# Where the first three transposed groups of each 512-token block are asked for

## The chip, the cores and the metric

One core of a Trainium2 chip runs the whole program. The metric is the device time of one execution in microseconds (us), as a median over several runs. The profile is of one execution of its own.

## The reference

```
p_packed = sm_attn(p, k, v)              # 8 batches, 8 heads, 576 tokens, head 64, 32 packs
x = sm_attn(q, p_packed, p_packed)       # -> 4608 tokens x 512
h = x @ w_in                             # 512 -> 1024
solu = h * softmax(h)
ln = (solu - mean) / sqrt(var + 1e-06) * g_ln
y = ln @ w_out                           # 1024 -> 512
m = max(y @ w1, y @ w2, y @ w3)          # 512 -> 768
out = m @ w_out2                         # 768 -> 512
```

Inputs and output are float32. Every matrix product outside the attention is made from operands split into a high and a low part, three matmuls for one.

## The kernel before, in words

The program has two stages. The first, up to some 530 us, makes the attention, `h`, the normalised activations and `y`. The second makes the three maxed products and the last product (lines 884 and 1146), and is a long run of matmuls. The change lies in the first.

**Tiles and blocks.** The 4608 tokens are 36 tiles of 128 (the loop `for t in range(nt)`, L1035). Four tiles are a block of 512 tokens, nine blocks in all. For each tile `tok_hidden` makes `h` (12 matmuls into two banks of PSUM, L633), and then VectorE and ScalarE turn it into `u`, the normalised activations, in a chain: the negated row maximum `nm` (L639, VectorE), the exponential (L641, ScalarE), the product `u` with its sum (L643, VectorE), `nmu` (L645), the squares (L647, ScalarE), the powers (L651 to L658, VectorE), and the final scaling of `u` (L659, ScalarE). When the four tiles of a block have their `u`, `y_transpose(j, kc)` transposes one group: the 128 columns number `kc` of the four `u` tiles, four 128x128 transposes on TensorE into one bank of PSUM (L700). ScalarE takes the high part from it (`lh`, L706), VectorE the low part (`ll`, L707), and the bank is free. There are eight groups in a block. `y_product` (L712) uses the group `kc` in two steps, one for each half of the output, six matmuls each (L725): 16 steps for a block.

**Banks.** The pool `ps_t` has four banks with one tag. The transposed groups share them with `mp` (L474, two banks for a set, evicted to `Mh` and `Ml`, L311 and L312), with `st` (L507, two banks for a set, evicted by two transposes of VectorE, L513), and with the transposes of queries and keys (L394, L488). `h` has two banks of its own.

**The order of work.** Each tile goes through a string of letters, for blocks in the middle `DFNTAHTTyTyDyTAFy`. `H` is `tok_hidden` of the tile itself; `y` brings the previous block's `y` to step 4i+4 at tile i of its block; `T` asks for one more transposed group of the previous block, if fewer than three are ahead of the `y` steps (`look=3`); `F` is a step of the attention of a later batch (`mp`, `st` and the VectorE work on it: `mx` L517, the difference L518, `sm` L521 to L523, `x` L524, the transposes L537); `D`, `W` and `A` are pieces of decoding weights (`dt` and `raw`, L123 to L139). Behind the fourth tile of each block, L1090 asks for the first three groups of that block at once. The order in which each engine then receives its instructions is set by a list scheduler. It is fixed when the program is built.

The seven places where this differs in the change are the ends of the tiles 7, 11, 15, 19, 23, 27 and 31. They are called the borders 1 to 7 here. They lie in the trace near 142, 193, 250, 301, 357, 408 and 458 us.

Of the kernel before, what the change touches and what calls it, by code (L numbers as in the profile page):

```python
# [57 lines left out]
def kernel(  # L58
# [155 lines left out]
    def decode_w_out(n, raw):  # L214

        t = lt_p.tile([P, TB], F32, tag="lh", name="dt")
        wt = lt_p.tile([P, TB], F32, tag="ll", name="wt")
        for f in decode(wt, raw, t, wt if CFG['l1'] == 'g' else None, ENG[CFG['d1']]):
            f()
        wv = wt.rearrange("r (k f) -> r k f", k=2)  # L220
        nc.scalar.copy(woh[:, 2 * n:2 * n + 2, :HM], wv)
        nc.gpsimd.tensor_tensor(
            out=wol[:, 2 * n:2 * n + 2, :HM], in0=wv, in1=f32(woh[:, 2 * n:2 * n + 2, :HM]), op=ALU.subtract
        )
        ready.update({(0, 2 * n), (0, 2 * n + 1)})

    def decode_w_out2(kc):

        t, start, rest = decode_piece(words(w_out)[kc * P:(kc + 1) * P, HM:, :])

        def arithmetic():
            rest()
            nc.scalar.copy(woh[:, kc, HM:], t)
            nc.gpsimd.tensor_tensor(out=wol[:, kc, HM:], in0=t, in1=f32(woh[:, kc, HM:]), op=ALU.subtract)
            ready.add((1, kc))

        return start, arithmetic
# [13 lines left out]
    def decode_w2(w, dst, r0, f):  # L251
        t, start, rest = decode_piece(words(w)[r0:r0 + P, f:f + DC, :])

        def arithmetic():
            rest()
            nc.sync.dma_start(out=dst[r0:r0 + P, f:f + DC], in_=t)

        return start, arithmetic
# [58 lines left out]
    nt = NT // P  # L317
# [652 lines left out]
    def load_w_out():  # L970
        if left:
            n = left.pop(0)
            raw = u_p.tile([P, DFF], F32, tag="u", name="raw").bitcast(I32)
            src = words(w_out)[2 * n * P:2 * (n + 1) * P, :HM, :]
            nc.sync.dma_start(
                out=raw.rearrange("r (k c) -> r k c", k=2), in_=src.rearrange("(k r) f t -> r k (f t)", r=P)
            )
            raws.append((n, raw.rearrange("r (f t) -> r f t", t=2)))
# [15 lines left out]
    def filler():  # L994
        if fill:
            fill.pop(0)()

    def need(t):
        for _, _, b, _ in parts_of(t):
            while not packed[b].done.issuperset(('M1', f'X{unit_of(b, t % tiles)}')):  # L1000
                filler()
# [6 lines left out]
    def finish():  # L1008

        for f in dec.pop(0):  # L1010
            f()

    def step_y(j, most):
        n = done.get(j, 0)
        if j >= 0 and n < most:
            while divmod(n, KFF) not in ready:
                if n < KFF:
                    if not raws:
                        load_w_out()
                    decode_w_out(*raws.pop(0))  # L1020
                else:
                    while dec:
                        finish()
                    if divmod(n, KFF) not in ready:
                        dec.append([*decode_w_out2(todo2.pop(0))])
            y_product(j, n)
            done[j] = n + 1

    def step_t(j, most):
        n = turned.get(j, 0)  # L1030
        if j >= 0 and n < min(most, KFF):
            y_transpose(j, n)
            turned[j] = n + 1

    for t in range(nt):  # L1035
        if t == 4:
            first_h.close()
            ps_y = late.enter_context(tc.tile_pool(name="ps_y", bufs=1, space=PSUM, reuse_waits="tile"))
        j, i = t // 4 - 1, t % 4
        for x in CFG['s0'][t] if j < 0 else CFG['s3' if t >= CFG['t3'] else 's2' if j else 's1']:  # L1040
            if x == 'H':
                need(t)
                tok_hidden(t)
            elif x == 'D':
                while dec:
                    finish()
                if raws:
                    decode_w_out(*raws.pop(0))
                elif t >= CFG['th'] and not left:
                    if todo2:  # L1050
                        dec.append([*decode_w_out2(todo2.pop(0))])
                    elif todo:
                        dec.append([*decode_w2(*todo.pop(0))])
                    elif todo3:
                        todo3.pop(0)()
            elif x == 'W':
                while dec:
                    finish()
                if todo3:
                    todo3.pop(0)()  # L1060
            elif x == 'A':
                for d in dec:
                    if len(d) == 2:
                        d.pop(0)()
            elif x == 'F':
                filler()
            elif x == 'L':
                load_w_out()
            elif x == 'N' and t % tiles in (3, 8) and nxt < B:
                while fill:  # L1070
                    filler()
                nb = packed[nxt] = Packed(nxt)
                nb.load(0)
                nb.load(1)
                fill += nb.steps()
                nxt += 1
            elif x == 'y':
                step_y(j, 4 * i + 4)
            elif x == 'T':
                step_t(j, done.get(j, 0) + CFG['look'])  # L1080
        if t % tiles in (3, 8) and nxt < B and (j < 0 or 'N' not in CFG['s1']):
            while fill:
                filler()
            nb = packed[nxt] = Packed(nxt)
            nb.load(0)
            nb.load(1)
            fill += nb.steps()
            nxt += 1
            filler()
        if i == 3:  # L1090
            for _ in range(CFG['look']):
                step_t(t // 4, CFG['look'])
    while fill or todo or dec or todo3:
# [162 lines left out]
```

## Time and profile before

| what | us |
|---|---|
| median of three runs | 1087.03 (1086.87 to 1087.38) |
| the profiled execution, its own time | 1080.05 |
| span of the profile | 1078.3 |
| mean granted clock of TensorE | 0.988 |
| PE busy, whole span | 1035.2 |
| VectorE busy, whole span | 713.0 |

The profiled execution is 6.98 us shorter than the median of the runs. A difference worked out in the profile is therefore put on its own 1080.05 us, and the same difference on the median. What lies outside the span is 1.75 us.

### The profile page before, as it was taken

Reading aid. Unit: us, or ns where it says so; the run is one execution under the profiler, and the core shown is the slowest. Engines: PE = TensorE matmul, PEld = TensorE weight load, DVE = VectorE, ACT = ScalarE, POOL = GpSimd, SP = SyncE. Lnnn points to the kernel's source line nnn. Section 1 sums busy time; section 2 is a strip of 40 time slices with the busy share of each in tenths; the row PEclk is TensorE's granted clock in tenths of the full one; section 3 lists DMA queues with packets and bytes.
Section 4 is the critical chain, followed back from the end, with each engine's and each line's share of the span. In section 5 each row is a group of like instructions: output and inputs, shape, how many; then the busy total and the mean of one; then the engine's idle time right before and its main releaser. Section 6 shows DMA issues by size and latency. Waiting matters only on the chain.

```text
span 1078.3 us, 18180 instructions
## 1 busy us (share of the span) xinstructions
PE 1035.2 (96%) x6624; PEld 881.1 (82%) x6624; DVE 713.0 (66%) x1434; ACT 482.4 (45%) x938; POOL 275.6 (26%) x296
## 2 busy tenths in 40 slices
PE   7779999999999999999999999999999999999997
PEld 6547667676767777777998899999989999999996
DVE  4697896979787896756888646625735754662560
ACT  6597666666666666576233421321331142132113
POOL 3342321111111121142585510410230041031002
PEclk8899999999999999999999999999999999999999
DMA  8853536564554623346564644543444453433411
GB/s 260 189 131 97 162 101 180 139 163 139 136 158 138 185 87 98 104 135 240 179 232 160 190 129 125 158 129 123 147 138 139 147 176 109 127 118 117 126 50 59
DMA packets 139528, 154.28 MB, mean 143 GB/s; under 512 B 51888, under 2 KB 92336, under 8 KB 139440
## 3 DMA queue, kind: packets, MB, share of 16 engines
q1 hardware_dynamic: 139440, 153.14, 48.6%
q8 instruction: 52, 0.85, 0.3%
q14 instruction: 36, 0.29, 0.1%
HBM read 116.92 MB, written 36.18 MB: 142 GB/s over the span
## 4 chain that ended last, share of the span: by engine, by line
PE 51%; DVE 2%; issue 1%; POOL 1%; DMA 1%; ACT 1%; DVEq 0%; ACTq 0%; POOLq 0%
PE m L884 33%; PE o L1146 13%; PE y L725 4%; PE h L633 1%; DVE wt L784 1%; DMA wt<-wdram 0%; PE tp L700 0%; DVE r L892 0%; POOL w2l L757 0%; DMA wt<-wodram 0%; DVE kept L892 0%; ACT u L659 0%; POOL hl L948 0%; POOL t1l L852 0%; DVE t L834 0%
## 5 line engine op out<-in xcount | busy, mean ns | idle before, releaser
L725 PE MATMUL y<-lh,woh 128*128 128x512 f32 x288 | 118.0, 413 | 0.6 <-ACT lh L706 0.6
L725 PE MATMUL y<-ll,woh 128*128 128x512 f32 x288 | 115.0, 399 | 0.0
L725 PE MATMUL y<-lh,wol 128*128 128x512 f32 x288 | 114.2, 397 | 0.0
L892 DVE TENSOR_TENSOR u<-m,q 128x384 f32<-128x384 f32 x54 | 29.9, 554 | 126.4 <-PE m L884 65.5
L917 ACT COPY q<-m 128x384 f32<-128x384 f32 x54 | 26.0, 481 | 178.4 <-PE m L884 178.4
L948 POOL TENSOR_TENSOR hl<-cur,hh 128x384 fp32r<-128x384 f32 x36 | 40.7, 1133 | 235.7 <-ACT hh L947 235.7
L139 POOL TENSOR_TENSOR wt<-raw 128x256 f32<-128x256 f32 x56 | 35.6, 636 | 228.2 <-DVE raw L136 130.3
L1146 PE MATMUL o<-w2h,hl 128*128 128x512 f32 x216 | 84.7, 392 | 0.6 <-POOL hl L948 0.6
L1146 PE MATMUL o<-w2l,hh 128*128 128x512 f32 x216 | 84.4, 391 | 0.0
L1146 PE MATMUL o<-w2h,hh 128*128 128x512 f32 x216 | 84.1, 389 | 0.0
L633 PE MATMUL h<-Mh,ah 128*128 128x512 f32 x160 | 67.5, 422 | 2.0 <-DVE u L643 1.5
L633 PE MATMUL h<-Mh,al 128*128 128x512 f32 x160 | 65.3, 408 | 0.0
L725 PEld LDWEIGHTS y<-lh,woh 128*128 128x128 f32 x288 | 53.8, 188 | 14.0 <-issue 1.4
L633 PE MATMUL h<-Ml,ah 128*128 128x512 f32 x160 | 64.9, 406 | 0.0
L725 PEld LDWEIGHTS y<-lh,wol 128*128 128x128 f32 x288 | 54.2, 188 | 12.1
L884 PE MATMUL m<-b22h,s 128*128 128x384 f32 x216 | 63.6, 335 | 0.0
L884 PE MATMUL m<-t1h,s 128*128 128x384 f32 x216 | 63.6, 334 | 0.0
L884 PE MATMUL m<-t2h,s 128*128 128x384 f32 x216 | 63.5, 334 | 0.0
L884 PE MATMUL m<-t3h,s 128*128 128x384 f32 x216 | 63.5, 334 | 0.0
L725 PEld LDWEIGHTS y<-ll,woh 128*128 128x128 f32 x288 | 54.4, 189 | 10.9 <-issue 0.5
L892 DVE TENSOR_TENSOR kept<-r,kept 128x384 f32<-128x384 f32 x72 | 58.4, 812 | 2.4
L707 DVE SCALAR_TENSOR_TENSOR ll<-tp,g_sb,lh 128x512 fp32r<-128x512 f32 x72 | 52.1, 743 | 11.8 <-ACT lh L706 11.7
(209 smaller groups left out, 2749.9 us busy)
## 6 DMA issues: line engine op xcount, KB each, us to landing
s<-sdram SPq DMA_DIRECT2D x188, 256.0 KB, 2.9
kt<-in_k_dram SPq DMA_DIRECT2D x16, 576.0 KB, 5.3
vt<-in_v_dram SPq DMA_DIRECT2D x16, 576.0 KB, 4.8
ydram<-yt SPq DMA_DIRECT2D x36, 256.0 KB, 2.5
raw<-in_moe_w_dram SPq DMA_DIRECT2D x36, 256.0 KB, 2.8
b<-ydram SPq DMA_DIRECT2D x24, 384.0 KB, 4.3
out_dram<-ob SPq DMA_DIRECT2D x36, 256.0 KB, 2.0
qtl<-in_q_dram SPq DMA_DIRECT2D x56, 128.0 KB, 2.9
```

The source lines that it names most:

```text
L139: add.tensor_tensor(out=dst, in0=f32(hi), in1=f32(lo), op=ALU.add)
L633: nc.tensor.matmul(h[:, n, :], lhsT=x, rhs=m[:, g, n * 512:(n + 1) * 512], start=(i == 0), stop=(i == len(ops) - 1),)
L707: last[nc.vector] = nc.vector.scalar_tensor_tensor(out=ll, in0=tp, scalar=gc, in1=f32(lh), op0=ALU.mult, op1=ALU.subtract)
L725: nc.tensor.matmul(ys[half][m], lhsT=w[:, kc, ms], rhs=x, start=(kc == 0 and i == 0), stop=(kc == KFF - 1 and i == 2),)
L784: nc.vector.tensor_tensor(out=out, in0=x, in1=y, op=op)
L884: nc.tensor.matmul(out, lhsT=w, rhs=y, start=start and i == 0, stop=i == len(ops) - 1, skip_group_check=not start,)
L892: mark[0] = nc.vector.tensor_tensor(**what)
L917: mark[1] = nc.scalar.copy(q, ba)
L948: nc.gpsimd.tensor_tensor(out=hl, in0=t, in1=f32(hh), op=ALU.subtract)
L1146: nc.tensor.matmul(ops[i], lhsT=x[:, ts], rhs=w, start=(c == 0 and n == 0), stop=(c == KF2 - 1 and n == 2),)
```

## The change

The line that asks for three groups behind a block's fourth tile now does so only for the first block (t = 3) and the last (t = 35). For the seven blocks between, the first three `T` of the next tile's string find no group yet, and ask for them: the first ahead of `H` of that tile, the second and the third behind it, and ahead of the first `y`. Nothing is computed more or less.

```
-        if i == 3:
+        if i == 3 and (t == 3 or t == nt - 1):
             for _ in range(CFG['look']):
                 step_t(t // 4, CFG['look'])
```

VectorE at border 1, around the evictions of the first five groups. `ll` are the low parts of the groups, `nm`, `u` and `nmu` belong to the next tile, `x` and `sm2` to the attention, `dt` and `raw` to decoding. The groups four and five are `ll_1938` and `ll_1969` in both orders. Before:

```order
L707 SCALAR_TENSOR_TENSOR ll_1876<-tp_1870,g_sb_119,lh_1875 128x512
L523 RECIPROCAL sm2_1826<-sm2_1826 128x20
L131 SCALAR_TENSOR_TENSOR raw_1784<-raw_1784,dt_1786 128x256
L524 TENSOR_TENSOR x_1809<-x_1809,sm2_1826 128x640
L134 TENSOR_SCALAR dt_1786<-raw_1784 128x256
L537 STREAM_TRANSPOSE y_1835<-x_1809 128x320 x2
L136 SCALAR_TENSOR_TENSOR raw_1784<-raw_1784,dt_1786 128x256
L639 TENSOR_REDUCE nm_1910<-h_1897 128x1
L707 SCALAR_TENSOR_TENSOR ll_1938<-tp_1932,g_sb_119,lh_1937 128x512
L128 TENSOR_SCALAR dt_1887<-dt_1887 128x256
L707 SCALAR_TENSOR_TENSOR ll_1969<-tp_1963,g_sb_119,lh_1968 128x512
L643 SCALAR_TENSOR_TENSOR u_1912,su_1914<-h_1897,u_1912 128x1024
```

Now:

```order
L639 TENSOR_REDUCE nm_1892<-h_1879 128x1
L537 STREAM_TRANSPOSE y_1835<-x_1809 128x320 x2
L707 SCALAR_TENSOR_TENSOR ll_1912<-tp_1906,g_sb_119,lh_1911 128x512
L643 SCALAR_TENSOR_TENSOR u_1894,su_1896<-h_1879,u_1894 128x1024
L707 SCALAR_TENSOR_TENSOR ll_1921<-tp_1915,g_sb_119,lh_1920 128x512
L645 TENSOR_SCALAR nmu_1898<-su_1896 128x1
L707 SCALAR_TENSOR_TENSOR ll_1938<-tp_1932,g_sb_119,lh_1937 128x512
L128 TENSOR_SCALAR dt_1860<-dt_1860 128x256
L707 SCALAR_TENSOR_TENSOR ll_1969<-tp_1963,g_sb_119,lh_1968 128x512
```

The second and third group are now evicted behind the next tile's `nm`, and the tile's `u` (L643) stands ahead of the third, fourth and fifth group instead of behind the fifth.

TensorE at border 2, directly behind the last `y` steps of the block before. Before:

```order
L700 MATMUL tp<-ident,u 128x128 x12
L474 MATMUL mp<-w_in_sb,ppT 32x512 x8
L507 MATMUL st<-qT,ppT 32x320 x8
L633 MATMUL h<-Mh,ah 128x512
L633 MATMUL h<-Ml,ah 128x512
L474 MATMUL mp<-w_in_sb,ppT 32x512 x8
L507 MATMUL st<-qT,ppT 32x256 x8
```

Now:

```order
L474 MATMUL mp<-w_in_sb,ppT 32x512 x8
L507 MATMUL st<-qT,ppT 32x320 x8
L633 MATMUL h<-Mh,ah 128x512
L474 MATMUL mp<-w_in_sb,ppT 32x512 x8
L507 MATMUL st<-qT,ppT 32x256 x8
L633 MATMUL h<-Ml,ah 128x512
L633 MATMUL h<-Mh,al 128x512
L633 MATMUL h<-Mh,ah 128x512
L633 MATMUL h<-Ml,ah 128x512
L633 MATMUL h<-Mh,al 128x512
L700 MATMUL tp<-ident,u 128x128 x4
```

The twelve transposes no longer stand ahead of the two sets of `mp` and `st`: both sets come first, with one `h` product between them, and the first group follows behind the sixth `h` product.

VectorE at border 3, from the next tile's `nm` to the eviction of the fifth group. The fourth group is `ll_3308`, the fifth `ll_3339`; `u` is the next tile's, `raw` and `dt` belong to decoding, the rest to the attention. Before:

```order
L639 TENSOR_REDUCE nm_3280<-h_3267 128x1
L521 TENSOR_REDUCE sm2_3254<-x_3237 128x2x8
L707 SCALAR_TENSOR_TENSOR ll_3308<-tp_3302,g_sb_119,lh_3307 128x512
L522 TENSOR_SCALAR sm2_3254<-sm2_3254 128x2x8
L134 TENSOR_SCALAR dt_3486<-raw_3484 128x256
L523 RECIPROCAL sm2_3254<-sm2_3254 128x2x8
L643 SCALAR_TENSOR_TENSOR u_3282,su_3284<-h_3267,u_3282 128x1024
L524 TENSOR_TENSOR x_3237<-x_3237,sm2_3254 128x2x256
L645 TENSOR_SCALAR nmu_3286<-su_3284 128x1
L136 SCALAR_TENSOR_TENSOR raw_3484<-raw_3484,dt_3486 128x256
L537 STREAM_TRANSPOSE y_3261<-x_3237 128x256 x2
L707 SCALAR_TENSOR_TENSOR ll_3339<-tp_3333,g_sb_119,lh_3338 128x512
```

Now:

```order
L639 TENSOR_REDUCE nm_3262<-h_3249 128x1
L521 TENSOR_REDUCE sm2_3227<-x_3210 128x2x8
L707 SCALAR_TENSOR_TENSOR ll_3282<-tp_3276,g_sb_119,lh_3281 128x512
L522 TENSOR_SCALAR sm2_3227<-sm2_3227 128x2x8
L707 SCALAR_TENSOR_TENSOR ll_3291<-tp_3285,g_sb_119,lh_3290 128x512
L523 RECIPROCAL sm2_3227<-sm2_3227 128x2x8
L643 SCALAR_TENSOR_TENSOR u_3264,su_3266<-h_3249,u_3264 128x1024
L524 TENSOR_TENSOR x_3210<-x_3210,sm2_3227 128x2x256
L645 TENSOR_SCALAR nmu_3268<-su_3266 128x1
L707 SCALAR_TENSOR_TENSOR ll_3308<-tp_3302,g_sb_119,lh_3307 128x512
L537 STREAM_TRANSPOSE y_3234<-x_3210 128x256 x2
L707 SCALAR_TENSOR_TENSOR ll_3339<-tp_3333,g_sb_119,lh_3338 128x512
```

The second and third group (`ll_3282`, `ll_3291`) have moved in behind `nm`, `u` stands ahead of the fourth too, and the pieces of decoding (L134, L136, and L131 some rows ahead) have gone from the stretch; they come behind the fifth group now.

## Rows read from the trace of the kernel before

**Rows 1.** Part 1 of the page: busy time, share of the span and instructions.

```profile
PE 1035.2 (96%) x6624; PEld 881.1 (82%) x6624; DVE 713.0 (66%) x1434; ACT 482.4 (45%) x938; POOL 275.6 (26%) x296
```

**Rows 2.** Stretches: length, PE, PEld, DVE, ACT, POOL busy (count), PEclk, DMA share, GB/s.

```profile
140.00:150.00 10.00, 7.89 (x34) 6.17 (x33) 9.41 (x22) 7.19 (x12) 2.40 (x5) 0.83 0.27 93
193.00:213.00 20.00, 19.72 (x158) 12.45 (x157) 19.27 (x44) 13.25 (x28) 3.25 (x3) 1.00 0.51 136
250.00:270.00 20.00, 19.56 (x138) 12.71 (x137) 19.03 (x43) 12.35 (x23) 2.81 (x5) 1.00 0.48 136
357.00:377.00 20.00, 19.19 (x169) 14.03 (x169) 16.95 (x46) 13.68 (x26) 2.45 (x4) 1.00 0.70 191
```

**Rows 3.** TensorE's timeline, border 1: start, us, instruction, count, idle before and releaser.

```profile
142.78 0.55 PE L700 MATMUL tp<-ident,u 128*128 128x128 f32 x3 [1.75 <-DVE x L513]
143.69 1.33 PE L700 MATMUL tp<-ident,u 128*128 128x128 f32 x5 [0.36 <-ACT u L659]
```

**Rows 4.** Timeline of VectorE, border 1.

```profile
148.11 0.82 DVE L521 TENSOR_REDUCE sm<-x 128x20 f32<-128x640 f32 x1 [0.40 <-ACT x L519]
...
156.27 1.23 DVE L643 SCALAR_TENSOR_TENSOR u<-h,u 128x1024 f32<-128x1024 f32 x1 [0.35 <-ACT u L641]
```

**Rows 5.** Timeline of TensorE, border 2.

```profile
192.94 1.47 PE L700 MATMUL tp<-ident,u 128*128 128x128 f32 x12
194.34 1.04 PE L474 MATMUL mp<-w_in_sb,ppT 64*32 64x512 f32 x2
195.66 1.09 PE L474 MATMUL mp<-w_in_sb,ppT 64*32 64x512 f32 x14 [0.28 <-DVE ll L707]
...
197.68 0.50 PE L633 MATMUL h<-Mh,ah 128*128 128x512 f32 x1
```

**Rows 6.** Timeline of TensorE, the same set away from a border.

```profile
435.08 1.09 PE L474 MATMUL mp<-w_in_sb,ppT 64*32 64x512 f32 x16
...
436.64 0.50 PE L633 MATMUL h<-Mh,ah 128*128 128x512 f32 x1
```

**Rows 7.** Timeline of VectorE, border 2: decoding, attention.

```profile
200.66 0.42 DVE L131 SCALAR_TENSOR_TENSOR raw<-raw,dt 128x256 int32<-128x256 int32 x1
...
204.86 0.28 DVE L134 TENSOR_SCALAR dt<-raw 128x256 int32<-128x256 int32 x1
...
205.25 0.36 DVE L136 SCALAR_TENSOR_TENSOR raw<-raw,dt 128x256 f32<-128x256 uint32 x1
...
210.24 0.67 DVE L517 TENSOR_REDUCE mx<-x 128x16 f32<-128x512 f32 x1
...
211.08 0.68 DVE L518 TENSOR_TENSOR x<-x,mx 128x512 f32<-128x512 f32 x1
```

**Rows 8.** Timeline of TensorE, border 3.

```profile
251.57 1.04 PE L474 MATMUL mp<-w_in_sb,ppT 64*32 64x512 f32 x2
...
254.68 0.50 PE L633 MATMUL h<-Mh,ah 128*128 128x512 f32 x1
```

**Rows 9.** Timeline of TensorE, border 7.

```profile
461.88 0.55 PE L700 MATMUL tp<-ident,u 128*128 128x128 f32 x3 [1.36 <-ACT u L659]
```

**Rows 10.** Stretches with the granted clock, columns as in rows 2.

```profile
140.00:143.50 3.50, 1.58 (x8) 0.81 (x6) 3.31 (x12) 3.12 (x5) 1.83 (x3) 1.00 0.10 32
143.50:147.00 3.50, 3.31 (x13) 2.94 (x14) 3.50 (x7) 2.99 (x7) 0.15 (x2) 0.52 0.45 155
460.90:464.30 3.40, 2.42 (x14) 2.00 (x14) 0.83 (x2) 3.40 (x7) 1.88 (x2) 1.00 0.68 226
```

**Rows 11.** Timeline of TensorE inside a block: third group behind a set.

```profile
325.57 0.60 PE L700 MATMUL tp<-ident,u 128*128 128x128 f32 x4
```

**Rows 12.** Timeline of VectorE, the same place.

```profile
323.78 0.74 DVE L707 SCALAR_TENSOR_TENSOR ll<-tp,g_sb,lh 128x512 fp32r<-128x512 f32 x1
...
327.90 1.18 DVE L643 SCALAR_TENSOR_TENSOR u<-h,u 128x1024 f32<-128x1024 f32 x1
329.02 0.77 DVE L513 STREAM_TRANSPOSE x<-st 128x256 f32<-128x256 f32 x2
```

## Prediction

> **What bounds the kernel now.** I read the page's first part first: TensorE is busy for 1035.2 of 1078.3 us [rows 1], so time can be won or lost only where TensorE waits. The change touches seven short places, and the share of the whole span says nothing about them. So I looked at stretches around the borders next [rows 2]. At border 1 TensorE is busy for 7.89 of 10 us and VectorE for 9.41; at borders 2 and 3 VectorE is busy for 19.27 and 19.03 of 20 us, at border 5 for 16.95. The reader is to see that the first three borders stand on VectorE: there a change in the order helps only if VectorE ends something sooner that TensorE needs. At border 5 VectorE has 3 us to spare, and I take borders 4 and 6, with the same kinds of work, to be like it.
>
> Then I read TensorE's timeline for what it waits for at the borders. At border 1 the first group's transposes wait 1.75 us for an L513, which frees a bank, and 0.36 us for the last tile's `u` [rows 3]. At border 2 the three groups take 1.47 us, and the next `mp` then waits until the groups are evicted: from its first matmul (194.34) to the first `h` product (197.68) it is 3.34 us, with an `ll` as releaser [rows 5]. The same set of `mp` and `st` away from a border needs 435.08 to 436.64, 1.56 us [rows 6]. So the banks that the three groups hold cost 3.34 - 1.56 = 1.78 us there. At border 3 it is 251.57 to 254.68, 3.11 us, so 1.55 us too many [rows 8]. At border 7 the wait is 1.36 us for `u` [rows 9].
>
> **The change, border by border.** No instruction of weight is added or taken away; no DMA is moved on purpose, and the pieces of decoding that slip behind the groups feed weights that are used much later. So the cost is in order alone. What I follow is the moment at which VectorE ends the eviction of the fifth group: the work that TensorE has behind it waits for that bank or for that `ll`, while a gap that TensorE has earlier in the same stretch is only filled or shifted.
>
> Border 1. The first group stays where it was on TensorE, so its waits of 1.75 and 0.36 us stay [rows 3]. The second and third go behind `h`. VectorE gets `u` (L643, 1.23 us) ahead of the third to fifth eviction, where it stood behind the fifth [rows 4]. Against that VectorE had 0.40 us of idle time in this stretch, ahead of `sm` [rows 4], which the pieces of decoding pulled ahead can fill. Sum: 1.23 - 0.40 = +0.8 us. The ends: 0 if the product steps hide it, and 1.23 + 0.35 = +1.6 us if VectorE also waits 0.35 us in front of `u`, as it does now [rows 4], with the evictions queued behind it.
>
> Border 2. The 1.78 us in front of the first set go away, since both sets now come ahead of the groups. But VectorE was not idle in those 1.78 us; it was evicting the groups that it now evicts later. What counts is its list up to the fifth eviction. Into it come `mx` and the difference of the second unit, 0.67 + 0.68 = 1.35 us; out of it go three pieces of decoding, 0.42 + 0.28 + 0.36 = 1.06 us [rows 7]. Sum: +0.3 us. The ends: -1.78 us if TensorE's wait was the whole cost, and +1.35 us if decoding's place is taken by waits for TensorE.
>
> Border 3. The same three pieces, 1.06 us by the durations of border 2 [rows 7], go out, and nothing comes in. In the new order the evictions stand closely behind `nm` and may wait for ScalarE's `lh`, so I take half: -0.5 us. The ends: -1.55 us [rows 8] and 0.
>
> Borders 4 to 6. The order changes in the same way, but VectorE has 20 - 16.95 = 3.05 us to spare in 20 [rows 2], more than the 1.23 us that `u` can put in front of an eviction [rows 4]. That slack hides it: 0. If the cover were gone, it would be up to 1.23 us each. Border 7. VectorE is far from full, and TensorE's 1.36 us are for `u` of the last tile [rows 9], which no move of transposes makes earlier. Three `h` products take the place of six transposes ahead of that wait; six transposes are half of 1.47 us [rows 5], so the term lies within 0.7 us on either side. I take 0.
>
> The sum is 0.8 + 0.3 - 0.5 = +0.6 us: on the profiled execution's own 1080.05 us that makes 1080.65, on the median of 1087.03, which is 6.98 us above it, **1087.6 us**. A measurement of this kernel can tell about 0.2% from no change, which is 2.2 us, so faster is below 1084.9 and slower above 1089.2.
>
> **The rivals.** *The banks decide.* If TensorE's waits at borders 2 and 3 are the whole cost and VectorE catches up later, 1.78 + 1.55 = 3.3 us go away [rows 5, 6, 8], and nothing is paid at border 1: 1087.0 - 3.3 = 1083.7 us. For it speaks that an `ll` releases the second `mp` [rows 5]. Against it speaks that VectorE is full for 19 of 20 us there [rows 2], so a bank that comes free sooner for one is taken from another. The Trainium skill ("Perfetto Trace Analysis", section "Optimization Strategy") says that the same gap repeating on the engine that should be saturated can mean that there isn't enough PSUM for the next tile; by that rule this change, which hands the banks to `mp` and `st` first, would gain the 3.3 us. The trace agrees that the gap repeats at two borders, but not at border 1, where the groups stay first. I give it 0.2.
>
> *The clock drops.* With no groups in front, TensorE at borders 2 and 3 comes to the second set sooner and waits for VectorE's `Ml`. At border 1 the waits of 1.75 and 0.36 us [rows 3] are followed by a stretch at half the clock: granted 0.52 from 143.5 to 147.0, of which TensorE was busy for 3.31 us [rows 10]. At full clock that work would take half, so a drop costs about 1.7 us. At border 7 a wait of 1.36 us was followed by none: the clock stays at 1.00 [rows 10]. [...] One drop gives 1087.6 + 1.7 = 1089.3 us, two give 1091.0. It speaks against it that `h` products stand between the two sets and can be put to use. I give it 0.2.
>
> *A group waits for a bank that comes late.* In a block's middle a third group started at 325.57, straight behind an `ll` (323.78), though an `st` held its bank until an L513 at 329.02 [rows 11, 12]: banks go round in the order in which they come free. If at border 2 the third group got the bank of the second `st` instead, it would wait for the L513 behind `u`, up to 329.02 + 0.77 - 325.57 = 4.2 us: 1091.8 us. The rows of the sibling speak against it; 0.08. *The change moves nothing:* the order on the engines shows that it does, so no chance is left for it.
>
> **How the numbers follow.** The forecast has 0.52, with a range of its own from 1086.0 to 1089.0 (the ends of border 3, -1.55 instead of -0.5, and of borders 1 and 2, +1.6 and +1.35 instead of +0.8 and +0.3, not all at once). The banks have 0.2 at 1083.7, the clock 0.2 between 1089.3 and 1091.0, the late bank 0.08 at 1091.8. The range of 8 in 10 takes in the forecast, nearly all of the banks' rival and the clock's: 1083.3 to 1091.2. Faster: the banks' rival and a little of the forecast's lower edge, 0.22. Slower: the clock, the late bank and the upper edge of the forecast, 0.31. Within 0.2%: 0.47.
>
> **What would show it.** In the profile after: at border 1 the first group's two waits unchanged, and the fifth `ll` some 0.8 us later than before; at border 2 no `ll` as releaser of an `mp`, 1.6 us instead of 3.3 from `mp` to `h`, but a new wait of `mp` for an `Ml` in the second set, and VectorE as full as before; at border 3 the next set a little earlier; at borders 4 to 6 TensorE's busy time the same within 0.3 us. It is wrong if VectorE's busy share at borders 2 and 3 falls while TensorE ends sooner (the banks), if a stretch with a granted clock near 0.5 appears near 195 or 253 (the clock), or if borders 4 to 7 move by more than a microsecond in sum: then the slack that I count on is not where the evictions need it.

## The result and the profile after

The change makes the kernel slower: 1089.97 us (median of 10 runs, 1088.79 to 1093.09) against 1085.64 us for the kernel before (10 runs, 1079.50 to 1087.50), medians 4.33 us apart. The ratio on record, which I use from here on, is 1.0062 with a 95% interval of 1.0045 to 1.0079; on 1085.64 us that is 6.7 us (4.9 to 8.6), so the distance of the medians lies just below the interval. The profiled execution of the change took 1088.79 us, with a span of 1086.9 us.

The first part of the page of the kernel after, busy times of the engines:

```profile
PE 1035.5 (95%) x6624; PEld 880.4 (81%) x6624; DVE 713.8 (66%) x1434; ACT 481.9 (44%) x938; POOL 276.2 (25%) x296
```

As in [rows 1] the work is the same; what grew is the time in which TensorE waits. The stretches that answer to [rows 2] are put 1.4 to 6 us later, as the kernel after is late by then (columns as there: length, then busy time and count of PE, PEld, DVE, ACT, POOL, then PEclk, DMA share, GB/s):

```profile
141.40:151.40 10.00, 7.89 (x36) 6.03 (x35) 9.81 (x25) 7.18 (x12) 2.78 (x6) 0.83 0.29 92
196.10:216.10 20.00, 16.84 (x135) 11.01 (x135) 17.35 (x35) 11.70 (x25) 2.18 (x2) 1.00 0.42 113
254.90:274.90 20.00, 18.09 (x137) 11.89 (x136) 18.84 (x40) 12.87 (x23) 2.96 (x5) 1.00 0.42 120
363.00:383.00 20.00, 18.18 (x166) 13.60 (x167) 15.78 (x41) 13.40 (x26) 2.45 (x4) 1.00 0.60 167
```

At border 2 TensorE fell from 19.72 to 16.84 us of 20, and VectorE from 19.27 to 17.35: it is no longer full, and both wait. At border 5 TensorE fell by 1.0 us and VectorE by 1.2; at border 3 TensorE fell by 1.5 and VectorE by 0.2.

**Border 1, the kernel after.** TensorE's timeline (start, duration, instruction, count, idle before and releaser), as in [rows 3]:

```profile
144.18 0.55 PE L700 MATMUL tp<-ident,u 128*128 128x128 f32 x3 [1.76 <-DVE x L513]
145.09 0.42 PE L700 MATMUL tp<-ident,u 128*128 128x128 f32 x1 [0.36 <-ACT u L659]
...
154.28 0.50 PE L725 MATMUL y<-ll,woh 128*128 128x512 f32 x1 [0.91 <-DVE ll L707]
...
156.51 0.50 PE L633 MATMUL h<-Mh,ah 128*128 128x512 f32 x1 [0.45 <-DVE u L643]
```

VectorE's timeline beside it:

```profile
149.71 0.74 DVE L707 SCALAR_TENSOR_TENSOR ll<-tp,g_sb,lh 128x512 fp32r<-128x512 f32 x1
...
151.57 1.22 DVE L639 TENSOR_REDUCE nm<-h 128x1 f32<-128x1024 f32 x1
152.70 0.89 DVE L537 STREAM_TRANSPOSE y<-x 128x320 f32<-128x320 f32 x2
153.52 0.71 DVE L707 SCALAR_TENSOR_TENSOR ll<-tp,g_sb,lh 128x512 fp32r<-128x512 f32 x1
155.22 1.23 DVE L643 SCALAR_TENSOR_TENSOR u<-h,u 128x1024 f32<-128x1024 f32 x1 [1.00 <-ACT u L641]
```

The first group's two waits are the old ones. New are a product step that waits 0.91 us for the second group's `ll`, which stands behind `nm` and the attention's transposes, and 0.45 us of `h` for the tile's `u`, for which VectorE itself had waited 1.00 us.

**Border 2, the kernel after.** TensorE's timeline, then VectorE's:

```profile
196.14 1.09 PE L474 MATMUL mp<-w_in_sb,ppT 64*32 64x512 f32 x16
...
197.70 0.49 PE L633 MATMUL h<-Mh,ah 128*128 128x512 f32 x1
199.52 1.25 PE L474 MATMUL mp<-w_in_sb,ppT 64*32 64x512 f32 x9 [1.33 <-DVE Ml L312]
...
203.25 0.66 PE L700 MATMUL tp<-ident,u 128*128 128x128 f32 x4 [0.26 <-DVE Ml L312]
...
207.20 0.66 PE L700 MATMUL tp<-ident,u 128*128 128x128 f32 x4 [1.45 <-DVE ll L707]
```

```profile
202.52 1.28 DVE L312 SCALAR_TENSOR_TENSOR Ml<-mp,Mh 128x512 fp32r<-128x512 f32 x2
205.38 0.82 DVE L521 TENSOR_REDUCE sm<-x 128x20 f32<-128x640 f32 x1 [1.59 <-ACT x L519]
...
206.40 0.74 DVE L707 SCALAR_TENSOR_TENSOR ll<-tp,g_sb,lh 128x512 fp32r<-128x512 f32 x1
```

The old wait of `mp` for the groups is gone: `mp` to `h` takes 1.56 us, as in [rows 6], where [rows 5] had 3.34. The second set now waits 1.33 us for `Ml`, and the third group 1.45 us for the first group's `ll`. The first of these waits is not the loss: VectorE comes to the second `Ml` (202.52) 6.71 us behind the start of block 1's last product (195.81). In the kernel before, where that product starts at 192.70, it was 9.03 us:

```profile
201.73 1.28 DVE L312 SCALAR_TENSOR_TENSOR Ml<-mp,Mh 128x512 fp32r<-128x512 f32 x2
202.93 0.81 DVE L521 TENSOR_REDUCE sm<-x 128x20 f32<-128x640 f32 x1
```

So up to there the change is 2.3 us ahead. Then VectorE stands idle for 1.59 us in front of `sm`, which it did not do before, and waits for ScalarE's exponentials (`x`, L519). ScalarE's list tells why they are late. After, and below it SyncE's queue (SPq rows are issues of DMAs):

```profile
204.29 0.43 ACT L123 ACTIVATE dt<-raw 128x256 f32<-128x256 f32 x1 [1.92 <-DMA raw<-in_moe_w_out_dram]
204.63 0.72 ACT L519 ACTIVATE x<-x 128x640 f32<-128x640 f32 x1
205.26 1.25 ACT L706 ACTIVATE lh<-tp,g_sb 128x512 fp32r<-128x512 f32 x2
```

```profile
199.64 0.32 SPq L256 DMA_DIRECT2D wodram<-wt  x1
200.01 0.43 SPq L244 DMA_DIRECT2D raw<-in_moe_w_out_dram  x1
```

Before, the same two:

```profile
199.24 0.45 ACT L123 ACTIVATE dt<-raw 128x256 f32<-128x256 f32 x1 [1.33 <-DVE x L513]
200.00 1.09 ACT L311 ACTIVATE Mh<-mp 128x512 fp32r<-128x512 f32 x2 [0.31 <-PE mp L474]
```

```profile
194.65 0.45 SPq L244 DMA_DIRECT2D raw<-in_moe_w_out_dram  x1
...
198.37 0.33 SPq L256 DMA_DIRECT2D wodram<-wt  x1
```

VectorE had the difference (L518) ready for the exponentials at 202.59, and ScalarE had nothing to do from 202.37 on. But a piece of decoding (`dt`) stands ahead of them and waits 1.92 us for its load. In the kernel before it stood ahead of the second `Mh`, which then still waited for `mp`, so that its wait cost nothing. The load is late too: it is issued 4.20 us behind the start of block 1's last product, behind a store (L256) that waits for the piece that GpSimd finishes; before, it was issued ahead of that store, 1.95 us behind that product. The first group's `ll` comes at 206.40. It needs ScalarE's `lh`, which stands behind the exponentials and is done at about 205.9, so its place behind `sm` on VectorE accounts for half a microsecond at most.

**Behind border 5, the kernel after.** TensorE, VectorE, ScalarE, and SyncE's queue:

```profile
381.76 0.65 PE L700 MATMUL tp<-ident,u 128*128 128x128 f32 x4 [1.65 <-DVE Ml L312]
```

```profile
380.29 0.29 DVE L128 TENSOR_SCALAR dt<-dt 128x256 int32<-128x256 int32 x1 [1.20 <-ACT dt L123]
380.67 0.42 DVE L131 SCALAR_TENSOR_TENSOR raw<-raw,dt 128x256 int32<-128x256 int32 x1
381.02 1.28 DVE L312 SCALAR_TENSOR_TENSOR Ml<-mp,Mh 128x512 fp32r<-128x512 f32 x2
```

```profile
379.83 0.43 ACT L123 ACTIVATE dt<-raw 128x256 f32<-128x256 f32 x1 [2.47 <-DMA raw<-in_moe_w_dram]
380.16 1.07 ACT L311 ACTIVATE Mh<-mp 128x512 fp32r<-128x512 f32 x2
```

```profile
375.49 0.37 SPq L244 DMA_DIRECT2D raw<-in_moe_w_dram  x1
```

Read from the bottom: the load of a weight piece is issued at 375.49; ScalarE's first step of decoding it (`dt`, L123) waits for it until 379.83, 2.47 us; `Mh` stands behind `dt` on ScalarE, `Ml` behind the same piece's L128 and L131 on VectorE, and TensorE waits 1.65 us for `Ml` (0.33 in the second profile of the kernel before). It is border 2's form once more, with `Mh` in the place of the exponentials.

**The account.** To find where the time came in, I took from TensorE's timeline the start of the last `y` matmul of each block, and the distances between them. The table has these distances as differences, in us, from those of a second profile of the kernel before (first run below; its own distances stand in the second column). Each row holds one border and the product steps that follow it.

| border | before, again | first profile of before | change | change, again |
|---|---|---|---|---|
| up to border 1 | 141.31 | -0.68 | +0.73 | +4.40 |
| 1 | 52.35 | -0.28 | +1.43 | +0.91 |
| 2 | 57.22 | +0.02 | +1.94 | +2.22 |
| 3 | 51.73 | -0.52 | 0.00 | 0.00 |
| 4 | 56.51 | -0.06 | +0.33 | +0.82 |
| 5 | 50.81 | -0.37 | +1.71 | +1.40 |
| 6 | 49.71 | 0.00 | +0.42 | +0.38 |
| 7 | 38.63 | +0.01 | +0.44 | +0.43 |
| 1 to 7 | 356.96 | -1.20 | +6.27 | +6.17 |

The two profiles of the change agree within 0.1 us on the sum, 6.2 us; against the first profile of before it is 7.4 to 7.5 us. The ratio's 6.7 us lie between. What scatters is the time up to border 1, where the order is the same in both programs: it goes with the granted clock of the first 100 us (0.90 in the first profile of before, 0.81 in the second of the change).

Border 1 has to be read with the clock beside it. In both profiles of before and in the first of the change it fell to half there, in the second of the change it did not. One run below (borders 2 to 5) has the old order at border 1 and no drop, and took 51.16 us there; it is the only one of its kind. So the change costs 1.43 us at border 1 if the clock falls in both, and 53.26 - 51.16 = 2.1 us if it falls in neither; the 0.91 of the table mixes the two.

### The profile page after: what moved, and what is told of

Same layout as the page of the kernel before. It is cut to its first block, busy times and chain, and to the rows that moved or that the text cites. A ratio compares the mean times of both kernels' runs of the same rounds, so it can differ in the third digit from the quotient of the medians.

```text
span 1086.9 us, 18186 instructions
## 1 busy us (share of the span) xinstructions
PE 1035.5 (95%) x6624; PEld 880.4 (81%) x6624; DVE 713.8 (66%) x1434; ACT 481.9 (44%) x938; POOL 276.2 (25%) x296
## 4 chain that ended last, share of the span: by engine, by line
PE 51%; DVE 2%; POOL 1%; issue 1%; DMA 1%; ACT 1%; DVEq 0%; ACTq 0%; POOLq 0%
PE m L884 32%; PE o L1146 13%; PE y L725 4%; PE h L633 1%; DVE wt L784 1%; DVE r L892 0%; DVE kept L892 0%; POOL w2l L757 0%; PE tp L700 0%; DMA wt<-wdram 0%; DMA wt<-wodram 0%; ACT u L659 0%; POOL hl L948 0%; POOL t1l L852 0%; DVE t L834 0%
```

## The experiments

The 95% interval of a ratio is some 0.2% either way, or 2 us; the sums by border are therefore given with each. "Border" means the distance of the table, against the second profile of before.

**The kernel before, a second time.** No edit.

> The kernel before, unchanged, profiled a second time. It tells what of the 8.6 us between the two spans is scatter of the start. In the two profiles the kernel of the change is already 1.40 us later when the last y product of block 0 starts, before the first border. If that is scatter, this run's first 140 us differ from the other profile's by 0.5 us or more while every stretch between two borders from border 1 on repeats within 0.2 us, and the ratio is 1.000 within 0.002. If stretches behind border 1 differ by 0.5 us or more as well, the account by border can't be read from single profiles.

Ratio 1.0008 (0.9983 to 1.0033). The stretches repeat within 0.06 us at four of seven borders, and differ by 0.28, 0.52 and 0.37 us at the borders 1, 3 and 5. Up to border 1 it is 0.68 us. Border 3 is thus just over the half microsecond that the expectation named as a sign against reading single profiles. So a difference of about half a microsecond or less at a single border isn't read, save where several runs show the same.

**Border 1 alone.**

```
-        if i == 3:
+        if i == 3 and t != 7:
```

> Only border 1 as in the change, the others as before. Theory A (the later evictions stand in VectorE's list behind work of the next tile and of the attention that itself waits for ScalarE, and TensorE waits for them): the two new waits of the change's profile come back, about 0.9 us of a y product for an ll and 0.45 us of h for u, and from the first product of block 1 to its last TensorE takes 1.5 to 2 us more than before; time +1.7 us. Theory B (VectorE's list is full and only gets longer by u less an idle gap, as forecast): +0.8 us and VectorE without a gap of over 0.5 us. Theory C (the loss lies elsewhere or in the start): 0 to 0.3 us.

Ratio 1.0026 (1.0005 to 1.0046); border 1 costs +0.86 us, the borders behind it differ by at most 0.16. TensorE's timeline of this run:

```profile
148.50 0.50 PE L725 MATMUL y<-ll,woh 128*128 128x512 f32 x1 [0.52 <-DVE ll L707]
...
152.27 0.50 PE L725 MATMUL y<-ll,woh 128*128 128x512 f32 x1 [1.66 <-DVE ll L707]
```

The product steps wait for `ll` as theory A says, even longer (0.52 + 1.66 us); the net looks nearer to B's number. But in this run the clock did not fall at border 1 (1.00 from 145.0 to 148.5), TensorE was 1.66 us earlier at the first product, and gave that back in the waits. The run of borders 2 to 5 has the old order here and no drop either:

```profile
143.50:147.00 3.50, 3.24 (x19) 2.50 (x18) 3.50 (x6) 3.50 (x7) 0.00 (x0) 1.00 0.42 145
```

It was 1.10 us earlier at the first product and kept that. Against it border 1 costs 2.05 us, a little more than theory A's 1.5 to 2 us; B's +0.8 falls.

**Borders 2 and 3 alone.**

```
-        if i == 3:
+        if i == 3 and t not in (11, 15):
```

> Only borders 2 and 3 as in the change. Theory A: at border 2 TensorE waits 1.3 us for an Ml in front of the second set and 1.4 us for the ll of an earlier group in front of the third group, VectorE stands idle for about 1.6 us in between for the exponentials of ScalarE; net +1.7 to +2 us at border 2 and +0.5 at border 3, together +2.3 us. Theory B (VectorE is full, and only the fifth eviction counts): +0.3 and -0.5, together -0.2 us. The rival by banks: -3.3 us.

Ratio 1.0029 (1.0010 to 1.0049); border 2 +3.91, border 3 -0.03, all others within 0.2 us. TensorE's timeline, and the clock behind it (a stretch as above):

```profile
208.41 0.66 PE L700 MATMUL tp<-ident,u 128*128 128x128 f32 x4 [2.17 <-DVE ll L707]
```

```profile
209.20:212.60 3.40, 3.40 (x11) 2.62 (x10) 3.40 (x6) 1.69 (x3) 0.00 (x0) 0.50 0.00 0
```

The third group waits for the first one's `ll`, 2.17 us here, and then the clock was at half for 3.4 us; between the first and the middle product of block 2 that cost 1.43 us. Without the drop border 2 is at 2.5 us. Theory B and the rival by banks fall: border 2 loses, and VectorE is not full there.

**Borders 4 to 7 alone.**

```
-        if i == 3:
+        if i == 3 and t not in (19, 23, 27, 31):
```

> Only borders 4 to 7 as in the change. Theory A: VectorE and ScalarE have spare time there on average, but their lists shift the Ml and the key and query evictions: about +0.2 at border 4, +2.5 us between the first product of block 5 and the first of block 6, +0.4 each behind borders 6 and 7, together +3 us. Theory B (the slack hides it): 0 within 0.5 us. Theory C (most of what the two profiles differ by behind border 4 is scatter): 0 to 1 us, and the waits for kT and pT of ScalarE near 400 us not in the profile.

Ratio 1.0015 (0.9992 to 1.0037); the borders 4 to 7 are +0.38, -0.95, +0.07 and +0.45, together -0.05 us. Theory A falls for these borders: by themselves they cost nothing in sum. The 2.9 us that the whole change loses there (table, borders 4 to 7) must come from somewhere else. The `Ml` wait near 380 is 0.33 us here:

```profile
376.61 0.66 PE L700 MATMUL tp<-ident,u 128*128 128x128 f32 x4 [0.33 <-DVE Ml L312]
```

**The change, a second time.** No edit.

> The changed kernel, unchanged, profiled a second time. If the account is sound, the stretch from the last y product of block 0 to the first of block 3 again takes about 3.3 us more than in the kernel before (border 1 some +1.5, border 2 some +1.8), with an idle VectorE of over 1 us in front of sm at border 2. The 2 us that the first profile lost between the first and the last product of block 5 (an Ml wait of 1.65 us near 380 us, waits for kT and pT behind it) are the open point: the order of VectorE's list predicts that the 1.65 us come back, as a piece of decoding stands ahead of that Ml; scatter predicts that they don't.

Ratio 1.0092 (1.0063 to 1.0120) from 4 runs; this profile lost 4.40 us up to border 1, where the order is the old one, and 6.17 us behind it. The idle VectorE at border 2 is back (1.78 us), and behind border 5 so is the wait for `Ml`, 1.39 us:

```profile
385.43 0.66 PE L700 MATMUL tp<-ident,u 128*128 128x128 f32 x4 [1.39 <-DVE Ml L312]
```

So the loss in block 5 is no scatter; it belongs to the order of this program.

**All three groups ahead of `h`, behind the attention step.** Only in the first tile of blocks 2 to 8, against the change, where these strings are `DFNTAHTWTyTyyTWFy` and `DFNTAHTTyTyDyTAFy`:

```
+        if j > 0 and i == 0:
+            steps = 'DFNTTTAHWyTyyTWFy' if t >= CFG['t3'] else 'DFNTTTAHyTyDyTAFy'
```

> As the change, but the next tile asks for all three groups behind its attention step and ahead of h. The second and third group are then evicted ahead of the next tile's nm, while the sets of mp and st at border 2 still come first. If border 1's cost is the place of the evictions behind nm and u, border 1 costs 0 within 0.3 us (TensorE's order there is the old one). If border 2's cost is that the first eviction stands behind sm, which waits for the exponentials on ScalarE, border 2 still costs 1.5 to 2.5 us; if nm were its cause too, it costs 0 as well. Sum +1.5 to +3 us by the first, 0 by the second.

Ratio 1.0031 (1.0010 to 1.0052). Border 1 costs +0.14 us, border 2 still +2.32 (with a drop of the clock again), border 3 -0.66, border 5 +2.20. The clock fell at border 1 here as in the profiles of before, so this +0.14 stands against the first profile of the change with its +1.43: border 1's cost is that the second and third group come behind `h`, and their evictions behind `nm` and `u`. Border 2's is another one. At border 2 VectorE has the same idle time ahead of `sm`, 2.08 us, and ScalarE's `dt` waits 2.40 us for its load.

**One group early, two groups early.** The number in the range is 1, then 2, for the blocks between:

```
         if i == 3:
-            for _ in range(CFG['look']):
+            for _ in range(CFG['look'] if t in (3, nt - 1) else 1):
```

> One group is asked for directly behind the block's fourth tile, the second and third by the next tile. Border 1: the second group is back ahead of h and nm, the third behind; the wait of a y product for the second ll goes, so border 1 costs 0 to 0.8 us instead of 1.4 to 1.9. Border 2: the first eviction goes back into VectorE's idle time ahead of the first Ml, so the third group need not wait for it: +0.3 to +0.8 us instead of 1.8 to 2.5. If instead the whole cost came from mp's second set waiting for Ml with no groups in front of it, border 2 costs as much as in the change.

> Two groups are asked for directly behind the block's fourth tile, the third by the next tile. Theory A: two evictions use VectorE's idle time, the first set of mp finds two banks free (so the old 1.8 us of waiting at border 2 and 1.55 at border 3 go), and no y product waits for the third group's ll for long: between -1.5 and +0.5 us. If evictions behind nm cost whatever their number, +0.7 us or more, in steps of the number of groups that have been moved.

With one early: ratio 1.0015 (0.9994 to 1.0037), border 1 +0.45, border 2 +0.13, sum +0.87 us. VectorE evicts that one group ahead of the first `Ml`, between pieces of decoding, no third group waits, and `sm` comes without idle time in front of it:

```profile
200.97 0.43 ACT L123 ACTIVATE dt<-raw 128x256 f32<-128x256 f32 x1 [3.02 <-DMA raw<-in_moe_w_out_dram]
201.31 1.06 ACT L311 ACTIVATE Mh<-mp 128x512 fp32r<-128x512 f32 x2
```

```profile
203.58 0.81 DVE L521 TENSOR_REDUCE sm<-x 128x20 f32<-128x640 f32 x1
```

This does not show that the place of one eviction was the cause. The order of this run moves the piece of decoding as well: the load is issued 1.93 us behind the last product of block 1, and `dt` stands ahead of the second `Mh` again, as in the kernel before. It waits even longer, 3.02 us, but the exponentials follow as soon as VectorE has the difference ready. With two early: ratio 1.0007 (0.9992 to 1.0022), border 1 -0.30, border 2 +0.99, border 4 +1.50, border 5 -0.69, sum +1.13 us, above the -1.5 to +0.5 expected. That is no less than with one, so the cost doesn't go in steps of the groups moved; what this run waits for I have not followed.

**Borders 1 and 4 to 7; borders 2 to 5.**

```
+        if i == 3 and t not in (7, 19, 23, 27, 31):
```

```
+        if i == 3 and t not in (11, 15, 19, 23):
```

> Borders 1 and 4 to 7 as in the change, 2 and 3 as before. Theory D: the 2 to 2.9 us that the whole change loses in block 5, and that borders 4 to 7 alone do not, come from a piece of decoding (L128, L131) that the delay at border 2 has pushed on to a place directly ahead of an Ml near 380 us, where it waits for ScalarE's dt. In this kernel's order no such piece stands there, so block 5 costs 0 or gains 0.7 us as in the run of borders 4 to 7 alone; only border 1's 0.9 to 1.5 us are left: +1 to +1.5 us in all. Rival: borders 4 to 7 cost 2 to 3 us as soon as an earlier border has shifted them: +3.5 to +4.5 us.

> Borders 2 to 5 as in the change, 1, 6 and 7 as before. Theory D: the piece of decoding stands ahead of that Ml again, so TensorE waits there 1.2 to 1.7 us, and from the first to the last product of block 5 it takes 1.3 to 2 us more than before though border 6 is the old one. With border 2's 1.8 to 2.5 us: +3.5 to +4.5 us. Rival (the loss in block 5 is border 6 or 7's, or comes from border 1): block 5 within 0.3 us of before, +1.8 to +2.5 us in all.

The first: ratio 1.0019 (0.9999 to 1.0038), border 1 +0.86 (no drop of the clock), border 5 -1.12, sum +0.57 us. The second: 1.0056 (1.0035 to 1.0077), border 1 -1.19 (the old order, no drop), border 2 +4.00 (with a drop), border 5 +1.50, sum +4.95. So, as far as these runs go, block 5's loss needs border 2 or 3 moved together with 4 or 5, and neither border 1 nor border 6 or 7; theory D had said so from the order. ScalarE in the second run has the late piece ahead of `Mh` again:

```profile
377.32 0.44 ACT L123 ACTIVATE dt<-raw 128x256 f32<-128x256 f32 x1 [2.10 <-DMA raw<-in_moe_w_dram]
377.66 1.07 ACT L311 ACTIVATE Mh<-mp 128x512 fp32r<-128x512 f32 x2
```

**One more `D`.** Against the change:

```
+        if t == 18:
+            steps = steps + 'D'
```

> The change with one more D at the end of tile 18's string, so that decoding catches up by a piece. The order then has a piece (L128, L131) ahead of an Ml not in one place but in two: in tile 21 (near 325 us) and, as in the change, in tile 25 (near 380 us). Theory D: a new wait for that Ml of about 1 to 1.5 us near 325 us, which the change does not have, and the old one near 380: block 4 costs 1 to 1.5 us more than in the change. If decoding's place does not matter, block 4 is within 0.3 us of the change, and if only its lag mattered, block 5's loss goes.

Ratio 1.0074 (1.0053 to 1.0095). Border 2 is +4.40 (with a drop of the clock), the sum +9.21 us. Border 4 costs +1.94 us, against +0.33 and +0.82 in the change. `mp` waits 0.87 us for an `Ml` near 328, behind a piece of decoding that waits for ScalarE's `dt`:

```profile
328.12 1.26 PE L474 MATMUL mp<-w_in_sb,ppT 64*32 64x512 f32 x9 [0.87 <-DVE Ml L312]
```

```profile
326.56 0.39 DVE L128 TENSOR_SCALAR dt<-dt 128x256 int32<-128x256 int32 x1 [0.50 <-ACT dt L123]
```

That is less than the 1 to 1.5 us expected, and the change waits 0.45 us in this place already. Behind it the third group waits 0.58 us for an `ll`, which it does not do in the change; ahead of that `ll` VectorE waits 1.36 us for a `dt`, and this one 2.04 us for its load. Together 1.0 us of the 1.1 to 1.6 that are new.

Behind border 5 this run parts two things that come together in the change, the wait for `Ml` and a later one for the copy of `pT`. The change near 413, then this run, near 387 and 418:

```profile
412.69 0.43 ACT L123 ACTIVATE dt<-raw 128x256 f32<-128x256 f32 x1 [2.12 <-DMA raw<-in_moe_w_out_dram]
...
413.33 0.47 PE L394 MATMUL tp<-ident,kt 96*128 96x96 f32 x3 [0.73 <-ACT pT L306]
```

```profile
387.35 0.66 PE L700 MATMUL tp<-ident,u 128*128 128x128 f32 x4 [1.48 <-DVE Ml L312]
...
417.67 1.16 PE L394 MATMUL tp<-ident,kt 96*128 96x96 f32 x12
```

In the change a `dt` waits 2.12 us for its load with the copy of `pT` behind it, and TensorE waits 0.73 us for `pT`; here that wait is absent, and the wait for `Ml` is there. From the first to the middle product of block 5 this run loses 0.93 us (the change 1.01 and 0.75), from the middle to the last -0.09 (the change 0.98 and 0.93). So the wait for `Ml` is about half of block 5's loss, and what comes behind it near 413 is the other half.

**A version from the gains.** The kernel before, with border 5 as in the change and two groups early at border 1:

```
-        if i == 3:
-            for _ in range(CFG['look']):
+        if i == 3 and t != 23:
+            for _ in range(2 if t == 7 else CFG['look']):
```

> An attempt at a version that beats both: the kernel before, with border 5 as in the change and only two groups asked for directly at border 1. From the stretches of the runs so far: -0.3 us at border 1, -0.3 to -1 us around block 5, so -0.5 to -1.3 us in the profile's stretches, which the times (about 0.2%) can hardly tell from no change. If the gains seen in single stretches are given back in the next, 0.

Ratio 0.9988 (0.9967 to 1.0009), 1081.77 us against 1083.11: no difference that the times can tell. In the stretches it is -0.71 us, -0.67 of it at border 5; border 1's -0.48 between the first and the middle product was lost again ahead of it (0.21) and behind it (0.26).

**Border 2 in all runs that have the change's order there.** ScalarE's `dt` stands ahead of the exponentials in each of them. The last column is the time from the last product of block 1 to the first of block 2, less the 10.02 us of the second profile of before; all in us.

| run | `dt` waits for its load | VectorE idle ahead of `sm` | later at the first product |
|---|---|---|---|
| the change | 1.92 | 1.59 | 1.78 |
| the change, again | 2.12 | 1.78 | 1.99 |
| groups ahead of `h` | 2.40 | 2.08 | 2.24 |
| borders 2 to 5 | 2.63 | 2.31 | 2.56 |
| borders 2 and 3 | 2.64 | 2.30 | 2.50 |
| one more `D` | 2.99 | 2.66 | 2.85 |

The wait grows by 1.07 us from the first row to the last, and so does the delay; the two differ by 0.07 to 0.16 us in every row. So border 2's loss up to the first product is the wait of one piece of decoding for its load. If VectorE's idle time went, 0.16 to 0.25 us would be left; that is an estimate from the last two columns, and no run takes the piece away alone.

## Why the prediction was wrong

The time of 1089.97 us lies inside the range, but that is luck. The forecast was no change (+0.6 us), the kernel is 6.7 us slower, and the upper part of the range stood for a drop of the clock at borders 2 and 3 and for a late bank, neither of which made the loss.

The step that failed is the one that put decoding at nothing: that its pieces, where they slip, "feed weights that are used much later". It looked at who uses the result, not at what stands behind the piece in ScalarE's and VectorE's lists while it waits for its load. In the two profiles of the change that costs 1.8 and 2.0 us at border 2 (by the table of the waits; +0.3 forecast) and 1.7 and 1.4 us in block 5 (0 forecast). Point by point:

- **Border 1, +0.8 us forecast.** Measured 1.43 us where the clock falls with and without the change, 2.1 us where it falls in neither; the ends were 0 and 1.6. The step was right in kind (the evictions come behind work of the next tile; the fifth `ll` starts 15.92 us behind the last product of block 0, in the second profile of before 14.54) and its size too small; the eviction that TensorE waits for longest is the second group's, behind `nm`, not the fifth.
- **Border 2, +0.3 us forecast, 1.94 and 2.22 measured.** The sum took VectorE's durations alone, and took it for granted that VectorE has something to do. But VectorE's list is served in order, and so is ScalarE's: a `dt` without its load holds up the exponentials, the exponentials hold up `sm`, and VectorE stands idle for 1.59 us. A full engine became one that waits, 17.35 instead of 19.27 us of 20. The 1.78 us in front of the first set were won, as the rival by banks has it, and VectorE was 2.3 us ahead at the second `Ml`; the wait for the load took it back and more.
- **Border 3, -0.5 us forecast, 0.00 measured** against the second profile of before, +0.52 against the first, so a gain isn't seen and a small loss can't be excluded. TensorE waits 1.2 us for an `Ml` ahead of the first group; 0.33 us are won up to the first product and 0.41 lost behind it. It is at the upper end that I gave, or above it.
- **Borders 4 to 7, 0 forecast, 2.9 measured.** Alone they come to -0.05 us, but as +0.38, -0.95, +0.07 and +0.45 (and nearly so in the run with border 1), not as four zeros: the slack does not hide each of them, and the forecast of 0 is luck in part. With borders 2 or 3 moved too, a piece of decoding meets another neighbour: `Mh` on ScalarE and `Ml` on VectorE, with its load not yet landed, and later `pT`. The rows show the 1.65 us; the runs of parts show that borders 2 or 3 must be moved too; the run with one more `D` shows `Ml` without `pT`. The +0.4 us each at the borders 6 and 7 and the 0.3 to 0.8 at 4 are seen in both profiles and were not followed.
- **The rivals.** The banks alone would have won 3.3 us; the waits of `mp` for banks did go, and TensorE waited elsewhere. The Trainium skill ("Perfetto Trace Analysis", section "Optimization Strategy") says that a repeating gap on the engine that should be saturated can mean too little PSUM. The trace agrees as far as that goes: with the banks free, `mp` to `h` took 1.56 instead of 3.34 us. The rival of a late bank was right that the third group waits, but it waits for the first group's own `ll`, not for the L513 that I had named, and for 1.45 us, not up to 4.2. The drop of the clock did not come at borders 2 and 3 in the two profiles of the change; at border 2 it came in four other runs, and in three of them block 2 took 1.4 to 1.5 us longer from its first to its middle product.
- **The signs I had named.** The first group's waits at border 1, the 1.6 us from `mp` to `h` and the new wait for `Ml` came as written. "VectorE as full as before" was the sign that failed, and "borders 4 to 7 move by more than a microsecond" the one that I had given for being wrong.

## What to carry to other kernels

When work moves along a list that is served in order, don't count the list's length alone: ask of each instruction that comes to stand elsewhere whether it waits for another engine or for a load, and what stands behind it. Follow a wait up to its end, too. VectorE waited for ScalarE, ScalarE for a load, and the load stood behind a store in SyncE's queue; whoever stops at the first of these mends the wrong list. And a side job that slips (decoding here) is not free because its result isn't needed yet: it can block whatever comes behind it in its queues. When a trial run moves one thing, look whether the scheduler moved another with it: the run with one group early looked like proof that an eviction's place was the cause, and it had moved the load.

## What the runs showed of the hardware

Outside of the clock's drops, the stretches repeat closely from one execution to another: where the order is unchanged, most of the table's distances of 39 to 57 us agree within 0.1 us (a few differ by up to 0.5), so that a profile tells parts of a microsecond that ten timings can't.

ScalarE did not pass over an instruction that waits for a load: at border 2 the exponentials had their input at 202.59 and started at 204.63, directly behind the `dt` whose load they don't need. From the issue of a load to the `dt` that waits for it, it was 4.28 us there (200.01 to 204.29) and 4.34 us behind border 5 (375.49 to 379.83).

The clock's drops don't follow a wait by its length alone. At border 1 TensorE waits 1.73 to 1.76 us ahead of the first group in the two profiles of before, the two of the change, and the runs of border 1 alone and of borders 2 to 5. The clock then fell to half for 3.4 us in both profiles before and in the first of the change, and stayed at 1.00 in the other three. In the old order a drop made border 1 1.19 us longer (52.35 against 51.16), in the change 0.52 us (53.78 against 53.26), where the waits for `ll` are longer without a drop (0.52 and 1.67 us) than with it (0.91). At border 2 the third group's wait was 1.45 and 1.65 us in the two profiles of the change, with no drop, and 1.92 to 2.52 us in the four runs that had one.
